# Retention and feed-forward on one core: earlier PE transposes, twelve PE-turned units in the output bank, half-tile stores from the ScalarE queue

## The chip, the cores and the metric

The kernel runs on one core of a Trainium2 chip. The metric is the device time of one execution in microseconds (us). The kernel before took 355.55 us (median of 3 runs, 354.68 to 355.61). One further execution was recorded by the hardware profiler; every duration below comes from that one.

Engine names are those of the profile: PE is TensorE's matmul, PEld its weight load, DVE is VectorE, ACT is ScalarE, POOL is GpSimd, and SP is SyncE, which here only starts transfers. An engine name with a q (SPq, POOLq) stands for that engine's instruction queue.

## The reference

Two operators run one behind the other. The first is a causal linear attention with a decay per head (8 batches, 8 heads, 576 positions, 64 dims); the second is a feed-forward layer with an ELU between its two products:

```
ret = (q @ k.T / sqrt(64)) * gamma_h ** (i - j)   for j <= i, else 0
x   = ret @ v                     # 4608 tokens x 512
h   = x @ w_in                    # 512 -> 2048
g   = where(h > 0, h, exp(min(h, 0)) - 1)
out = g @ w_out                   # 2048 -> 512
```

Inputs, weights and output are float32 in DRAM. The kernel multiplies in bfloat16 and accumulates in float32.

## The kernel before

**Units.** The 4608 tokens are cut into 36 units of 128 tokens; a pair of batches is nine units, and u % 9 tells whether a unit starts a batch (0), straddles two (4) or ends one (8). Per unit the attention does the following. Three loads on SP's queue (`load`; six smaller ones where u % 9 is 4) bring q, k and v. `cast` makes q and k bfloat16 (tile qkn), and `scale_v` on POOL multiplies v by the key side of the decay (tile vn). `turn` brings q and k into the transposed layout (tile qkT): for units below `PE_TURNED` by eight PE transposes into a PSUM tile tr, copied out half by DVE and half by ACT, and for the others by one transposing DMA on SP's queue. `scores` (16 matmuls into the one bank sc), `masks` on DVE (sc to pt), `inter` and `intra` (both into the one bank o), `state` (bank st) and `state_out` (ACT, tile sb, which the next unit's `inter` reads) finish the attention; `put_x` on DVE scales bank o into the group's tile xt. `stretch(u)` issues `scores` of unit u+1, then `inter`, `state`, `intra` of u, `masks` of u+1, `put_x` and `state_out` of u.

**Groups.** The feed-forward part works on groups of units: units 0 to 3, then 4 and 5, then 6 and 7, then seven groups of four. `ffn1` takes one group and one block of hidden columns: PE into a bank (three banks with the tag ph, or the one bank pm where told so), ACT computes the exponential (tile e), POOL subtracts 1 (tile m), DVE takes max and min with the bank's content (tile g). Only then is the bank free. `ffn2` sums 16 blocks of g into bank pm, ACT copies it out and SP stores it. For group 0 alone `ffn2_half` does this in eight half tiles of 256 columns, since the weights arrive in halves.

**Order.** The order on every engine is that of the code; nothing reorders it. The parts are: a loop over units 0 to 3 with dummy matmuls between its steps (`dummy`); `ffn1` of group 0; eight `ffn2_half` with the attention of units 4 and 5 between them; a loop of eight `ffn1` of group 1 with units 6 and 7; and from g = 2 on a merged sequence of `ffn1` of group g and `ffn2` of group g-1, with a `stretch` at four places.

**Queues around the change.** In the loop over units 0 to 3 each unit's steps follow each other: cast, transposes, scores, masks, `intra`. Loads of units 4 to 7 are issued on SP inside `ffn1` of group 0, and the half-tile stores (L351) stand behind them on the same queue. The copies of half tiles out of PSUM (L350) use three output buffers (opool, tag ot), so the fourth copy waits for the first store to land. Transposing DMAs stand on SP's queue from unit 8 on.

## Time and profile before

| | |
|---|---|
| three runs, median (lowest to highest) | 355.55 us (354.68 to 355.61) |
| profiled execution | 354.05 us |
| its span in the trace | 352.3 us |
| PE busy | 314.5 us, 89% of the span |
| DVE, POOL, ACT busy | 191.5, 137.5, 130.9 us |
| transfers | 49.73 MB, mean 141 GB/s |

The span is what the trace shows from the first to the last instruction; the 1.75 us by which the execution is longer lie around it. PE's busy share is 90% or more in most of the 40 slices of the page, and lower between about 50 and 115 us; there the time before and behind a matmul has to be read, not the share. The table of stages (first group of rows below) cuts the span at the starts of the kernel's parts: 0 to 26.9 is the loop over units 0 to 3, 26.9 to 40.7 `ffn1` of group 0, 40.7 to 50.3 five half tiles of `ffn2`, 50.3 to 58.6 a stretch without PE work, 58.6 to 71.8 the other half tiles with units 4 and 5, 71.8 to 89.2 `ffn1` of group 1 with units 6 and 7, 89.2 to 114.7 the merged sequence for g = 2, and the rest the sequences for g = 3 to the end. In the rows of a timeline the first number is the start, the second the time taken, and brackets hold how long the engine had been idle before and what ended that.

### The profile page before, as it was taken

To read this page: it belongs to the slowest core of one execution; us is meant where nothing else is said; L and a number is where in the kernel's file an instruction comes from. 1 tells how busy PE (TensorE), PEld (TensorE's weight loads), DVE (VectorE), ACT (ScalarE), POOL (GpSimd) and SP (SyncE) were. 2 spreads that over 40 slices of the span, in tenths; PEclk is the share of its full clock that TensorE was granted. 3 is DMA by queue.
4 is the path that set the end of the run, shared out by engine and by line. 5 is a ranking of instruction groups with operands and counts; after the bars stand their busy time and mean duration, and the time that the engine had idled before them with its cause. 6 is when DMAs were issued, how large, how long until landed. Compare 5 with 4: busy or idle time off the path is not lost.

```text
span 352.3 us, 7014 instructions
## 1 busy us (share of the span) xinstructions
PE 314.5 (89%) x2746; PEld 164.7 (47%) x2782; DVE 191.5 (54%) x286; ACT 130.9 (37%) x234; POOL 137.5 (39%) x205
## 2 busy tenths in 40 slices
PE   8889973866975999999899989998999999999995
PEld 3444562755554444444444444443454444444442
DVE  2545701547466688566666656565657465444400
ACT  5325502334221454433334334433443344344411
POOL 4585521036233655434344433443344332333300
PEclk9999996989996999999999999999999999999999
DMA  9999997723999989876958794879677221000021
GB/s 174 185 156 199 195 204 159 154 72 76 206 198 224 198 183 188 175 172 150 179 137 160 167 187 121 180 152 191 139 160 152 60 68 54 31 30 32 30 89 60
DMA packets 154144, 49.73 MB, mean 141 GB/s; under 512 B 142848, under 2 KB 150016, under 8 KB 154112
## 3 DMA queue, kind: packets, MB, share of 16 engines
q1 hardware_dynamic: 147840, 45.10, 61.8%
q0 software_dynamic: 6272, 4.19, 8.2%
q8 instruction: 21, 0.34, 0.5%
q14 instruction: 11, 0.09, 0.1%
HBM read 36.70 MB, written 9.44 MB: 131 GB/s over the span
## 4 chain that ended last, share of the span: by engine, by line
PE 28%; issue 27%; POOL 15%; DVE 14%; DMA 6%; SPq 6%; ACT 1%; POOLq 0%; DVEq 0%; ACTq 0%
POOL m L311 12%; PE pm L326 12%; PE ph L304 9%; SPq L85 5%; DMA rv<-in_v_dram 5%; DVE pt L212 5%; PE dum L359 4%; DVE qkn L166 4%; POOL vn L175 3%; DVE g L313 3%; DVE xt L276 2%; DMA rqk<-in_k_dram 1%; PE sc L203 1%; SPq L191 1%; ACT qkT L189 1%
## 5 line engine op out<-in xcount | busy, mean ns | idle before, releaser
L313 DVE SCALAR_TENSOR_TENSOR g<-ph,m 128x512 bf16<-128x512 f32 x144 | 98.6, 689 | 98.8 <-POOL m L311 98.6
L311 POOL TENSOR_SCALAR m<-e 128x512 bf16<-128x512 f32 x144 | 89.7, 624 | 159.1 <-ACT e L309 156.6
L304 PE MATMUL ph<-xt,w_in_sb 128*128 128x512 bf16 (+1 forms) x619 | 144.4, 361 | 6.9 <-DVE xt L276 5.7
L309 ACT ACTIVATE e<-ph 128x512 f32<-128x512 f32 x144 | 86.0, 597 | 144.1 <-PE ph L304 142.5
L326 PE MATMUL pm<-w_out_sb,g 128*128 128x512 bf16 x501 | 127.6, 381 | 4.5 <-DVE g L313 2.6
L304 PEld LDWEIGHTS <-w_in_sb 128*128 128x128 bf16 x640 | 61.5, 99 | 68.0 <-issue 8.2
L326 PEld LDWEIGHTS <-g 128*128 128x128 bf16 x512 | 49.7, 98 | 62.2 <-issue 4.2
L175 POOL TENSOR_TENSOR vn<-rv,gk 128x512 bf16<-128x512 f32 x36 | 37.7, 1048 | 29.3 <-DMA rv<-in_v_dram 23.1
L212 DVE TENSOR_TENSOR pt<-sc,mask 128x1024 bf16<-128x1024 f32 x36 | 43.7, 1215 | 8.1 <-PE sc L203 8.1
L166 DVE CAST qkn<-rqk 128x1024 bf16<-128x1024 f32 x28 | 24.3, 867 | 9.5 <-DMA rqk<-in_k_dram 6.1
L276 DVE TENSOR_TENSOR xt<-o,gx 128x512 bf16<-128x512 f32 x36 | 24.4, 679 | 2.9 <-PE o L263 2.9
L203 PE MATMUL sc<-qkT 64*64 64x128 bf16 x576 | 15.3, 225 | 11.2 <-DMA qkT<-qkn 5.1
L336 ACT COPY ot<-pm 128x512 f32<-128x512 f32 x31 | 18.1, 585 | 16.9 <-PE pm L326 16.7
L203 PEld LDWEIGHTS <-qkT 64*64 64x64 bf16 x576 | 9.6, 107 | 25.9 <-issue 7.8
L359 PE MATMUL dum<-warm 128*128 128x512 bf16 x58 | 17.5, 438 | 1.9 <-DVE warm L108 1.3
L255 ACT CAST sb<-st 128x256 bf16<-128x256 f32 x32 | 11.9, 372 | 19.3 <-PE st L246 19.3
L345 PE MATMUL pmh<-w_out_sb,g 128*128 128x256 bf16 x128 | 15.9, 284 | 0.5 <-DVE g L313 0.5
L263 PE MATMUL o<-pt,vn 128*64 128x128 bf16 x288 | 14.7, 224 | 0.0
L345 PEld LDWEIGHTS <-g 128*128 128x128 bf16 x128 | 12.8, 102 | 3.0 <-DVE g L313 0.8
L187 PE MATMUL tr<-ident,qkn 128*128 128x128 bf16 x64 | 5.5, 231 | 8.3 <-ACT qkn L169 8.3
L229 PE MATMUL o<-qkT,sb 64*64 64x128 bf16 (+1 forms) x256 | 12.5, 217 | 0.3 <-DVE xt L276 0.2
L263 PEld LDWEIGHTS <-vn 128*64 128x64 bf16 x288 | 9.5, 112 | 2.2 <-issue 1.7
(42 smaller groups left out, 74.9 us busy)
## 6 DMA issues: line engine op xcount, KB each, us to landing
rqk<-in_q_dram SPq DMA_DIRECT2D x32, 256.0 KB, 3.7
rqk<-in_k_dram SPq DMA_DIRECT2D x32, 256.0 KB, 4.4
rv<-in_v_dram SPq DMA_DIRECT2D x32, 256.0 KB, 4.6
out_dram<-ot SPq DMA_DIRECT2D x32, 256.0 KB, 2.0
w_in_sb<-in_moe_w_in_dram POOLq DMA_DIRECT2D x4, 512.0 KB, 8.4
w_out_sb<-in_moe_w_out_dram POOLq DMA_DIRECT2D x4, 512.0 KB, 15.9
rqk<-in_q_dram SPq DMA_DIRECT2D x8, 128.0 KB, 4.2
rqk<-in_k_dram SPq DMA_DIRECT2D x8, 128.0 KB, 4.4
```

The costliest lines, as they stand in the source:

```text
L166: engs[0](n, src)
L175: nc.gpsimd.tensor_tensor(n, rv, gk[:, u % R].unsqueeze(2).to_broadcast([P, H, D]), ALU.mult)
L203: nc.tensor.matmul(sc[j * 64 : (j + 1) * 64, i, hp], t[r, 1, hp, j * 64 : (j + 1) * 64], t[r, 0, hp], start=(hp == 0), stop=(hp == HP - 1) ...
L212: nc.vector.tensor_tensor(pt.rearrange("p i h t -> p (i h) t"), scs[u].rearrange("p i h t -> p (i h) t"), m.unsqueeze(1).to_broadcast([P, ...
L276: nc.vector.tensor_tensor(xts[g][:, :, i * P : (i + 1) * P], os_[u], gx[:, :, s0 : s0 + P], ALU.mult)
L304: nc.tensor.matmul(ph[:, i * n : (i + 1) * n], w_in_sb[:, j, f : f + P], xts[g][:, j, :n], start=(j == 0), stop=(j == KJ - 1), skip_group_ ...
L309: nc.scalar.activation(e, ph, AF.Exp)
L311: nc.gpsimd.tensor_scalar(m, e, -1.0, 1.0, ALU.add, ALU.mult)
L313: nc.vector.scalar_tensor_tensor(gt_, ph, 0.0, m, ALU.max, ALU.min)
L326: nc.tensor.matmul(pm, gts[g, ft][:, it * P : (it + 1) * P], w_out_sb[:, ft], start=(ft == 0), stop=(ft == NFT - 1))
L345: nc.tensor.matmul(pm, gts[g, ft][:, it * P : (it + 1) * P], w_out_sb[:, ft, c * 256 : c * 256 + 256], start=(ft == 0), stop=(ft == NFT - 1),)
L359: nc.tensor.matmul(dum, warm[:, :P], warm, start=True, stop=True)
```

## The change

- In the loop over units 0 to 3 the next unit's casts and transposes stand between the current unit's `masks` and `intra`; there are fewer dummies. The four exponentials that make gx (`make_gx`) follow unit 0's casts on ACT. A one-element copy `seen` on POOL reads unit 3's q ahead of the first weight load.
- Units 4 to 11 (before: units 4 to 7) are turned on PE, and their tile tr now takes the one bank o instead of a ph bank (units 0 to 3 keep ph).
- Loads of units 4 to 11 (before: 4 to 7) are issued in one go.
- Half-tile stores and the stores of groups 1 and 2 go from SP's queue to ACT's; there are five output buffers instead of three.
- Units 4 to 11 are placed anew among the feed-forward steps.

```
-    PE_TURNED = 8
+    PE_TURNED = 12
...
-    opool = ctx.enter_context(tc.tile_pool(name="opool", bufs=3))
+    opool = ctx.enter_context(tc.tile_pool(name="opool", bufs=5))
...
-    for hp in range(HP):
-        nc.scalar.activation(gx[:, hp, :S], px, AF.Exp, bias=bx, scale=lgx[:, hp : hp + 1])
-    nc.gpsimd.tensor_copy(gx[:, :, S:], gx[:, :, 0:64])
+
+    def make_gx():
+        for hp in range(HP):
+            nc.scalar.activation(gx[:, hp, :S], px, AF.Exp, bias=bx, scale=lgx[:, hp : hp + 1])
+        nc.gpsimd.tensor_copy(gx[:, :, S:], gx[:, :, 0:64])
...
-    def turn(u):
+    def turn(u, bank=None):
...
-            ps = ps_h.tile([P, 2, HP, P], BF16, name="tr", tag="ph")
+            pool, tag = bank or (ps_o, "o")
+            ps = pool.tile([P, 2, HP, P], BF16, name="tr", tag=tag)
...
-            nc.sync.dma_start(out[i0 : i0 + P, :], ot)
+            (nc.scalar if g < 3 else nc.sync).dma_start(out[i0 : i0 + P, :], ot)
...
-        nc.sync.dma_start(out[u * P : (u + 1) * P, c * 256 : c * 256 + 256], ot)
+        nc.scalar.dma_start(out[u * P : (u + 1) * P, c * 256 : c * 256 + 256], ot)
...
-    nload = [8]
+    nload = [12]
...
     dummy(18)
+    cast(0, A, V)
+    make_gx()
+    scale_v(0)
+    turn(0, (ps_h, "ph"))
+    dummy(2)
     for u in range(4):
-        cast(u, A, V if u == 0 else G)
-        if u == 3:
-            load_w_in(0)
-        scale_v(u)
-        turn(u)
-        dummy(3)
         scores(u)
         inter(u)
         state(u)
-        dummy(5)
         masks(u)
+        if u < 3:
+            if u == 2:
+                G(seen, raws[3][0][0:1, 0, 0, 0:1])
+                load_w_in(0)
+            cast(u + 1, A, A if u == 2 else G)
+            scale_v(u + 1)
+            dummy(3)
+            turn(u + 1, (ps_h, "ph"))
+        else:
+            dummy(4)
         intra(u)
-        dummy(3)
         put_x(u)
         state_out(u)
+        dummy(2)
...
         if ft == 5:
             load(4, nc.vector)
-            load(5)
-            load(6)
-            load(7)
+            for u in range(5, 12):
+                load(u)
...
     prep(5, A, V)
     ffn2_half(1, 1)
     scores(4)
+    inter(4)
+    state(4)
     masks(4)
+    ffn2_half(2, 1)
+    intra(4)
+    put_x(4)
+    state_out(4)
     turn(5)
-    load_next()
-    load_next()
-    ffn2_half(2, 1)
-    stretch(4)
+    ffn2_half(3, 1)
+    scores(5)
     prep(6, A, V)
-    ffn2_half(3, 1)
+    inter(5)
+    state(5)
+    masks(5)
+    dummy(4)
+    intra(5)
+    put_x(5)
+    state_out(5)
     turn(6)
-    stretch(5)
     for i in range(8):
         ffn1(1, 2 * i, (ps_m, "pm") if i % 4 == 3 else None)
         if i == 0:
             prep(7, A, V)
+            scores(6)
+            masks(6)
+        if i == 1:
+            inter(6)
+            state(6)
+            intra(6)
+            put_x(6)
+            state_out(6)
         if i == 2:
             turn(7)
...
+    turn(8)
...
+        if g == 2:
+            at = [5, 9, 12, 14]
         for n, (what, gg, s) in enumerate(seq):
...
+            if g == 2 and n in (3, 7, 10):
+                turn(nxt[0] + 1)
             if nxt and n in at:
                 u = nxt.pop(0)
-                prep(u + 3, V)
+                prep(u + 2, V) if u < 10 else None
+                if u >= 9:
+                    prep(u + 3, V)
                 load_next()
                 stretch(u)
```

Three places show what this moves. The names are those of the code above; a row is one instruction, with x for equal ones in a row.

The first place is DVE in the loop over units 0 to 3, from unit 0's copy of tr on. Before:

```order
L188 COPY qkT<-tr 128x512
L212 TENSOR_TENSOR pt<-sc,mask 128x1024
L276 TENSOR_TENSOR xt<-o,gx 128x4x128
L188 COPY qkT<-tr 128x512
L212 TENSOR_TENSOR pt<-sc,mask 128x1024
```

And after:

```order
L191 COPY qkT<-tr 128x512
L215 TENSOR_TENSOR pt<-sc,mask 128x1024
L191 COPY qkT<-tr 128x512
L279 TENSOR_TENSOR xt<-o,gx 128x4x128
L215 TENSOR_TENSOR pt<-sc,mask 128x1024
```

The next unit's copy of tr (second L191) moved ahead of the current unit's `put_x` (L279).

The second place is the half-tile stores. Before, they stand on SP behind the loads of unit 7:

```order
L85 DMA rqk<-in_q_dram 128x8x64
L85 DMA rqk<-in_k_dram 128x8x64
L85 DMA rv<-in_v_dram 128x8x64
L351 DMA out_dram<-oth 128x256 x6
L85 DMA rqk<-in_q_dram 128x8x64
```

After, they stand on ACT between its copies and casts. This piece starts behind the sixteen exponentials of group 0; in brackets is what an instruction waits for, where DMAHW is the count of transfers that share one of eight semaphores:

```order
L354 DMA out_dram<-oth 128x256 [waits DMAHW3_49,DVE_49]
L353 COPY oth<-pmh 128x256 [waits PE_49]
L354 DMA out_dram<-oth 128x256 [waits DMAHW5_49,Activation_49]
L354 DMA out_dram<-oth 128x256 [waits DMAHW7_49,DVE_49]
L353 COPY oth<-pmh 128x256 [waits PE_49]
L354 DMA out_dram<-oth 128x256 [waits DMAHW1_49,Activation_49]
L171 CAST qkn<-rqk 128x512 [waits DMAHW4_49]
L354 DMA out_dram<-oth 128x256 [waits DMAHW3_49,DVE_49]
L192 COPY qkT<-tr 128x512 [waits DVE_49]
```

The stores no longer follow the loads, but unit 4's cast of q (L171) and its copy of tr (L192) now follow four and five stores on ACT, and each store waits for an earlier transfer of the same semaphore.

The third place is DVE in the sequence for g = 2, around `stretch(9)`. Before, one cast precedes each `masks`:

```order
L313 SCALAR_TENSOR_TENSOR g<-ph,m 128x512
L166 CAST qkn<-rqk 128x1024
L212 TENSOR_TENSOR pt<-sc,mask 128x1024
L276 TENSOR_TENSOR xt<-o,gx 128x4x128
```

After, unit 9's `put_x` (second L279 below) stands behind two casts and unit 10's `masks`:

```order
L279 TENSOR_TENSOR xt<-o,gx 128x4x128
L316 SCALAR_TENSOR_TENSOR g<-ph,m 128x512
L191 COPY qkT<-tr 128x512
L316 SCALAR_TENSOR_TENSOR g<-ph,m 128x512
L168 CAST qkn<-rqk 128x1024 x2
L215 TENSOR_TENSOR pt<-sc,mask 128x1024
L279 TENSOR_TENSOR xt<-o,gx 128x4x128
L316 SCALAR_TENSOR_TENSOR g<-ph,m 128x512
L191 COPY qkT<-tr 128x512
```

The last L191 is the copy of unit 11's tr; its transposes on PE write bank o, which the `put_x` ahead of it has to read first.

## Rows read from the trace of the kernel before

**Rows 1.** Stages: length; busy PE, PEld, DVE, ACT, POOL (xcount); clock, DMA share, GB/s.
```profile
0.00:26.90 26.90, 23.05 (x242) 11.45 (x247) 11.58 (x36) 10.47 (x18) 15.20 (x29) 1.00 1.03 172
26.90:40.70 13.80, 13.72 (x63) 6.26 (x64) 9.10 (x15) 8.92 (x15) 8.63 (x14) 1.00 1.38 196
40.70:50.30 9.60, 9.06 (x81) 7.64 (x79) 3.16 (x6) 1.00 (x3) 2.28 (x3) 1.00 1.21 194
50.30:58.60 8.30, 0.04 (x1) 0.00 (x0) 0.18 (x1) 0.89 (x2) 2.08 (x2) 0.77 1.01 209
58.60:71.80 13.20, 10.83 (x168) 8.79 (x169) 7.32 (x12) 4.28 (x9) 0.00 (x0) 0.89 0.66 143
71.80:89.20 17.40, 13.11 (x143) 9.63 (x143) 9.91 (x15) 6.45 (x12) 8.72 (x11) 0.90 0.33 74
89.20:114.70 25.50, 18.85 (x247) 12.85 (x250) 15.39 (x20) 6.47 (x12) 9.05 (x12) 0.87 1.15 209
114.70:352.30 237.60, 225.87 (x1805) 108.06 (x1830) 134.87 (x183) 92.44 (x164) 91.49 (x135) 1.00 0.58 127
```

**Rows 2.** Timeline, 43 to 60 us: SP's last loads and first stores, and who waits.
```profile
47.55 1.04 POOL L175 TENSOR_TENSOR vn<-rv,gk 128x512 bf16<-128x512 f32 x1 [5.26 <-DMA rv<-in_v_dram]
...
53.79 9.38 SPq L351 DMA_DIRECT2D out_dram<-oth  x6
54.08 1.04 POOL L175 TENSOR_TENSOR vn<-rv,gk 128x512 bf16<-128x512 f32 x1 [1.92 <-DMA rv<-in_v_dram]
57.67 0.37 ACT L350 COPY oth<-pmh 128x256 f32<-128x256 f32 x1 [12.16 <-DMA out_dram<-oth]
...
58.62 1.03 PE L187 MATMUL tr<-ident,qkn 128*128 128x128 bf16 x8 [8.28 <-ACT qkn L169]
...
59.45 2.95 PE L345 MATMUL pmh<-w_out_sb,g 128*128 128x256 bf16 x16
...
63.14 1.91 PE L345 MATMUL pmh<-w_out_sb,g 128*128 128x256 bf16 x16
```

**Rows 3.** The w_out loads' line: first and last start, time to landing.
```profile
L100 POOL DMA_DIRECT2D w_out_sb<-in_moe_w_out_dram x4: 913/918/933, 21.2 to 23.8; - x4
...
DMA to landing us min/median/max: 13.0/15.9/20.6
```

**Rows 4.** Timeline of one unit in the loop over units 0 to 3.
```profile
14.22 0.42 PE L203 MATMUL sc<-qkT 64*64 64x128 bf16 x16 [0.49 <-ACT qkT L189]
...
14.69 1.23 DVE L212 TENSOR_TENSOR pt<-sc,mask 128x1024 bf16<-128x1024 f32 x1 [1.14 <-PE sc L203]
...
16.36 0.61 POOL L169 CAST qkn<-rqk 128x512 bf16<-128x512 f32 x1 [1.35 <-DMA rqk<-in_k_dram]
...
17.23 0.61 PE L187 MATMUL tr<-ident,qkn 128*128 128x128 bf16 x8
...
18.97 0.26 PEld L203 LDWEIGHTS <-qkT 64*64 64x64 bf16 x16 [0.98 <-ACT qkT L189]
```

**Rows 5.** Timeline, 87 to 115 us: PE's waits for a bank and for a transposing DMA.
```profile
87.45 1.89 PE L326 MATMUL pm<-w_out_sb,g 128*128 128x512 bf16 x7 [2.56 <-DVE g L313]
...
89.62 1.05 PE L304 MATMUL ph<-xt,w_in_sb 128*128 128x256 bf16 x8
...
109.17 0.64 PE L203 MATMUL sc<-qkT 64*64 64x128 bf16 x16 [5.05 <-DMA qkT<-qkn]
```

**Rows 6.** Groups by line over the span: busy, mean ns | idle before, releasers.
```profile
L313 DVE SCALAR_TENSOR_TENSOR g<-ph,m 128x512 bf16<-128x512 f32 x144 | 98.6, 689 | 98.8 <-POOL m L311 98.6
L311 POOL TENSOR_SCALAR m<-e 128x512 bf16<-128x512 f32 x144 | 89.7, 624 | 159.1 <-ACT e L309 156.6 <-DVE g L313 2.5
...
L166 DVE CAST qkn<-rqk 128x1024 bf16<-128x1024 f32 x28 | 24.3, 867 | 9.5 <-DMA rqk<-in_k_dram 6.1 <-DMA rqk<-in_q_dram 3.4
...
L189 ACT COPY qkT<-tr 128x512 bf16<-128x512 bf16 x8 | 4.7, 585 | 13.4 <-DVE qkT L188 13.4
...
L188 DVE COPY qkT<-tr 128x512 bf16<-128x512 bf16 x8 | 3.4, 422 | 5.7 <-PE tr L187 5.7
```

More of the change, by code (lines that the diff above doesn't have):

```diff
@@ L350, in ffn2_half @@
         (nc.scalar.copy if u % 2 else nc.vector.tensor_copy)(ot, pm)
-        nc.sync.dma_start(out[u * P : (u + 1) * P, c * 256 : c * 256 + 256], ot)
+        nc.scalar.dma_start(out[u * P : (u + 1) * P, c * 256 : c * 256 + 256], ot)
     V, A, G = nc.vector.tensor_copy, nc.scalar.copy, nc.gpsimd.tensor_copy
-    dum = ps_m.tile([P, 512], FP32, name="dum", tag="pm")
     def dummy(n):
+        dum = ps_m.tile([P, 512], FP32, name="dum", tag="pm")
         for _ in range(n):
@@ L374, in load_next @@
             nload[0] += 1
+    seen = const.tile([1, 1], FP32, name="seen")
     dummy(18)
-    for u in range(4):
-        cast(u, A, V if u == 0 else G)
-        if u == 3:
-            load_w_in(0)
-        scale_v(u)
-        turn(u)
-        dummy(3)
+    cast(0, A, V)
[3 more added lines that the diff above has]
+    dummy(2)
+    for u in range(4):
         scores(u)
@@ L426 @@
             prep(7, A, V)
+            scores(6)
[6 more added lines that the diff above has]
+            state_out(6)
         if i == 2:
             turn(7)
-        if i == 3:
-            stretch(6)
-            prep(8, V)
-            load_next()
-        if i == 5:
-            prep(9, V)
-            load_next()
-        if i == 7:
-            stretch(7, ahead=False)
-            prep(10, V)
-            load_next()
+        if i == 4:
+            scores(7)
+            masks(7)
+            prep(8, A, V)
+        if i == 6:
+            stretch(7, ahead=False)
+            prep(9, A, V)
+            load_next()
+    turn(8)
     for g in range(2, NG + 1):
@@ L457 @@
         at = [n for n, (what, gg, s) in enumerate(seq) if what and s % 4 == 3]
-        if g in (2, 3):
+        if g == 3:
             at = [len(seq) * (i + 1) // 4 - 1 for i in range(4)]
         at[-1] -= 3
+        if g == 2:
+            at = [5, 9, 12, 14]
         for n, (what, gg, s) in enumerate(seq):
```

## The prediction

> **What bounds the kernel now.** I read the table of stages first, since PE's share over the whole span hides where it waits. [rows 1] shows two kinds of stage. From 114.7 us to the end PE is busy 225.87 of 237.6 us at clock 1.00: PE sets the time, and the change touches this part only in its first stores. The seven stages ahead of that, 114.7 us, hold 88.7 us of PE work, some of it dummies and some at a low clock (0.77 to 0.90 in four of them). Everything the change can win lies there.
>
> Next I read the timeline where PE does nothing at all, 50.3 to 58.6 us. [rows 2]: PE's transposes of unit 4 wait 8.28 us for ACT's cast of unit 4's q. That cast has had its data since about 47.5 us (POOL scales unit 4's v, the last of its loads, at 47.55), but ACT works in order and stands at a half-tile copy, which waits 12.16 us for an output buffer. The buffer is freed by the first half-tile store, and SP issues that store at 53.79 only, behind the loads of unit 7. So a queue's order makes the hole, no amount of work.
>
> Then the loop over units 0 to 3. [rows 4]: from one scores (14.22) to the next (18.97) are 4.75 us, and what ends last is serial: scores, masks 1.23 us, `intra`, transposes at 17.23, two copies one behind the other (ACT's copy waits for DVE's each time: [rows 6], 13.4 us in 8), scores.
>
> Last, 71.8 to 114.7 us. [rows 5]: PE waits 2.56 us for bank pm (DVE's g frees it), and 5.05 us at 109.17 for a transposing DMA while the transfers are saturated (DMA share 1.15 in that stage, after 0.33 in the one before, [rows 1]).
>
> **The change, stage by stage.** Sums run against the profiled execution, 354.05 us with a span of 352.3.
>
> *Units 0 to 3.* The first scores stay where they are: the 18 dummies still stand ahead of unit 0's transposes, and the exponentials for gx end before ACT has to copy these. With the next unit's transposes under the masks a period becomes, on PE, scores 0.42, `inter` and `state` (half as many matmuls each) 0.35 each, three dummies 0.65 (13.8 us / 64 = 0.216 for a 128x512 matmul, [rows 1]), transposes 0.61: 2.4 us; then DVE's copy 0.42, ACT's copy 0.59 and hops of 0.1: 3.5 us instead of 4.75. The masks fit beside it (0.47 + 1.23 = 1.7). Three periods save 3.75, the shorter last unit 0.2. `ffn1` of group 0 starts at 22.9 instead of 26.9. The loads don't forbid it: unit 3's k is there at 16.4 ([rows 4], the cast that waited for its DMA), and unit 3's transposes come at 18. **-4.0** (bounds -3 to -4.8). `seen` makes POOL wait for unit 3's q, but POOL's next work waits for unit 3's v, which lands later: nothing; were it not so, the weights come late by a POOL step of 0.6 us.
>
> *`ffn1` of group 0 and five half tiles.* Same PE work, 13.8 + 9.6 us: they end at 46.3. The last weights landed at 44.4 (23.8 + 20.6, [rows 3]) and are needed from 45 on; the loads of units 4 to 11 now start 4.2 us earlier against them, so this is tight. **0** (bounds 0 to +2).
>
> *The hole.* The stores leave SP's order, and five buffers let the fourth copy go without any store. What is late next is unit 4 itself: its v landed at 47.55, with the transfers saturated (DMA share 1.21 to 1.38, [rows 1]), and beginning earlier gains little on a full path. Units then land every 3.3 us (unit 4's v used at 47.55, unit 6's at 54.08: [rows 2]). Against 46.3 I leave 1.5 us of the 8.3: **-6.8** (bounds -8.3, if unit 4 is there in time, to -3.3, if the early loads of units 5 to 7 and six stores of 128 KB hold it up). Each store also occupies ACT while it is issued; SP took 9.38 us for six, waits for their copies included, so at most 1.6 us for one. ACT hides that: it is busy 1.00 of 9.6 us in the stage of the five half tiles ([rows 1]). Without this cover eight issues would cost up to 12 us, which is rival D.
>
> *The other half tiles, units 4 and 5.* Three half tiles of 1.9 us, three turns (units 4, 5 and 6; 0.6 each, the last beside `put_x`), two attentions (scores 0.42, the other three steps 0.4 at most: 1.5 each), and at the end, with nothing beside them, unit 5's masks, and `put_x`, a DVE pass over the same elements as g (0.69): 5.7 + 1.2 + 3.0 + 1.2 less 0.6 for the steps under the masks + 0.7 = 11.2 instead of 13.2 us. 1.0 of it is the half tile that ran at a low clock right after the hole (2.95 against 1.91 us, [rows 2]). **-2.0** (bounds -2.6 to +1, where unit 5 or 6 lands late).
>
> *Group 1 with units 6 and 7.* PE work: 8 `ffn1` x 1.05, two attentions 3.1, two turns 1.2, two `ffn2` pieces 1.9: 14.6 us. The waits come from DVE, which serves g, casts, masks, `put_x` and now copies of tr. `intra` of unit 6 waits for masks behind a g and a cast (1.5), scores and `intra` of unit 7 wait 0.4 and 0.6, the transposes of unit 8 wait for unit 7's `put_x` in bank o (1.0), and bank pm for the last g (0.6). Together 18.6 us against 17.4: **+1.2** (bounds -2 to +3).
>
> *Sequence for g = 2.* Gone: the wait of 5.05 us for a transposing DMA, since units 8 to 11 need none and their loads fell into earlier stages. In its place PE transposes three times in bank o, where it waits for `put_x` of the unit before. PE work: 8 x 1.05 + 6 x 0.9 + four stretches 5.4 + scores 0.4 + three turns 1.8 = 21.4 us. Waits: unit 10's transposes for unit 8's `put_x` 1.0. Unit 11's transposes wait longest: from the end of `put_x` of unit 8, DVE does g 0.69, copy 0.42, g 0.69 (for which it waits some 2 us, since ACT's exponential and POOL's m of 0.62 come behind a `ffn1` that PE starts late), two casts of 0.87, masks 1.23, `put_x` 0.69, in all 7.5 us with hops, while PE has 4.8 us of work (0.6 + 1.05 + 0.9 + 1.2 + 1.05): 2.7. Then 0.9 at bank sc and o for unit 11 and 1.3 before group 3's first `ffn1`. Together 27.3 us against 25.5: **+1.8** (bounds -3 to +4). What such a bank costs no row before shows; the 2.56 us of [rows 5] for bank pm is nearest to the 2.7 that I take.
>
> *From 114.7 on.* Same instructions in the same order, loads equally far ahead; four stores of units 4 to 7 stand on ACT, beside 92 us of ACT's work in 237. **0** (bounds -0.5 to +1).
>
> Sum: -4.0 - 6.8 - 2.0 + 1.2 + 1.8 = -9.8, so 344.25 as a profiled execution. The median of the three runs lies 1.5 us above the profiled one, their lowest 0.6 above; I add about 1 and forecast 345 us.
>
> **Rule against the rows.** SP issues the first store at 53.79, after the loads ahead of it, while ACT has been waiting for that store for most of 12.16 us [rows 2]; by these rows another queue frees the store. The Trainium skill, page "DMA: Bandwidth & Descriptors", section "Issuing engines are not separate DMA queues", says that transfers started by different engines run on the same 16 DMA engines and interleave, so a second issuing engine saves issue time only. By that rule little of the 8.3 us would come back: with -1.5 in place of -6.8, some 350 us. The rows show what it leaves out, the place in an in-order queue.
>
> **Rivals.**
> (B) The bank waits of the two stages after 71.8 don't bite: DVE runs ahead, both stages take their PE work and half the waits (16.6 and 24.4 us). Then -5 more: 340 us. For it: DVE is busy only 9.91 of 17.4 and 15.39 of 25.5 us there [rows 1]. Against: the waits are chains, not load.
> (C) Transfers are the bound from 30 to 60 us: their share is above 1 already, and now eight units, weights and stores come at once. Weights +2, hole -3.3, next stage +0.5 instead of 0, -6.8, -2.0 lose 8 us of the gain: 353 us; half of that, 349. This is the mechanism for which the page above speaks.
> (D) Slower: ACT becomes the queue in which things stick. Each store on ACT waits for an earlier transfer of its semaphore, and unit 4's cast and copy stand behind it. If these transfers are loads of late units, ACT stands until they land: unit 8 lands at 54.1 + 2 x 3.3 = 60.7, unit 11 at 70.6. Transposes of unit 4 at 71 instead of 58.6 make +12.4; with -2.0 + 3.0 behind it 367 us. It decides against the change from about 57.5 us of landing on. Against it: counted through by their semaphores in the order after, the first store follows a load of unit 3, and the second to fourth follow loads of unit 4, which its cast has to wait for anyway.
> (E) The gain in the first units is eaten by the wait for weights and the hole closes only in part, 354.5 to 356.5 us.
>
> **How the numbers follow.** The forecast (own range 341 to 348.5) has 0.55, B (334 to 341) 0.18, C (348.5 to 354) 0.18, D 0.06, E 0.03. The likeliest's bounds and the near halves of B and C give 337.5 to 351, which leaves out the far end of B, the worst of C, D and E, 2 in 10. A measurement of this kernel tells about 0.3% (1.1 us) from no change. Faster: 0.55 + 0.18 + 0.17 = 0.90; same: E and a rest of C, 0.04; slower: 0.06.
>
> **What would show it.** Right: in the timeline after, `ffn1` of group 0 starts near 22.9 us with scores every 3.5 us; the transposes of unit 4 follow the fifth half tile within 2 us; no copy of a half tile waits for a store; group 1's `ffn1` starts at 57 to 60; PE waits for DVE's xt (`put_x`) ahead of the transposes of units 8, 10 and 11; the last part takes 237 to 238 us. Wrong: ACT idle before a store for several us (D), PE waiting for loads in the half tiles or at units 5 and 6 (C), or the two stages behind group 1's start taking under 41 us together (B). The forecast fails if the last part isn't the same length.

## The result, and the profile after

The changed kernel takes 345.73 us (median of 4 runs, 345.54 to 346.47), beside 355.12 us for the kernel before on the same chip: a ratio of 0.9741, 95% interval 0.9716 to 0.9765. That is faster, by 9.4 us; the forecast was 345.0, range 337.5 to 351. The profiled execution took 345.76 us with a span of 344.1, so the span is 8.2 us shorter than before.

The stages of the changed kernel, as [rows 1] has them of before (length; busy PE, PEld, DVE, ACT, POOL; clock, DMA share, GB/s). The cuts are at the same places: start of `ffn1` of group 0, first half tile, end of the fifth one, transposes of unit 4, `ffn1` of group 1, `scores(8)`, group 3. Two of them are early here: the first half tile starts at 36.93, not 36.46, and the fifth ends at 46.75, not 46.10.

```profile
0.00:22.66 22.66, 18.86 (x225) 9.56 (x226) 11.42 (x36) 10.89 (x19) 12.24 (x27) 1.00 1.07 171
22.66:36.46 13.80, 13.50 (x62) 6.06 (x62) 8.57 (x14) 8.49 (x15) 10.78 (x17) 1.00 1.33 199
36.46:46.10 9.64, 9.05 (x79) 7.50 (x78) 3.09 (x6) 1.81 (x4) 1.53 (x3) 1.00 1.33 199
46.10:47.70 1.60, 0.65 (x6) 0.34 (x4) 0.85 (x2) 0.62 (x1) 1.01 (x1) 1.00 1.19 312
47.70:59.40 11.70, 10.04 (x156) 7.97 (x157) 5.77 (x9) 3.69 (x8) 2.14 (x3) 1.00 1.04 248
59.40:78.10 18.70, 13.36 (x176) 9.60 (x175) 11.50 (x18) 8.37 (x16) 8.14 (x11) 1.00 1.18 217
78.10:106.36 28.26, 20.41 (x273) 13.79 (x273) 18.51 (x24) 8.52 (x16) 10.57 (x13) 0.94 0.46 95
106.36:344.10 237.74, 228.06 (x1832) 108.16 (x1831) 134.12 (x182) 91.72 (x163) 90.75 (x134) 1.00 0.58 126
```

The stretch without PE work (8.30 us in [rows 1]) is 1.60 us long by these cuts, and PE works in 0.65 us of it. The loop is 4.3 us shorter, the stages with units 6 to 11 are longer (18.7 and 28.3 us instead of 17.4 and 25.5), and the last part is as long as before. The clock, which was 0.77 to 0.90 in four stages of before, is 1.00 in all but one.

The timeline around the former hole, which answers to [rows 2] (start, length, what; in brackets the idle time before and what ended it):

```profile
40.05 0.38 ACTq L354 DMA_DIRECT2D out_dram<-oth  x1
...
41.74 2.97 ACTq L354 DMA_DIRECT2D out_dram<-oth  x2
...
44.83 0.37 ACT L353 COPY oth<-pmh 128x256 f32<-128x256 f32 x1 [3.12 <-PE pmh L348]
...
46.14 0.43 DVE L171 CAST qkn<-rqk 128x512 bf16<-128x512 f32 x1 [2.63 <-DMA rqk<-in_k_dram]
...
46.69 1.04 POOL L177 TENSOR_TENSOR vn<-rv,gk 128x512 bf16<-128x512 f32 x1 [8.20 <-DMA rv<-in_v_dram]
46.69 0.34 ACTq L354 DMA_DIRECT2D out_dram<-oth  x1
...
47.07 0.62 ACT L171 CAST qkn<-rqk 128x512 bf16<-128x512 f32 x1 [1.87 <-DMA rv<-in_v_dram]
...
47.74 0.62 PE L190 MATMUL tr<-ident,qkn 128*128 128x128 bf16 x8 [0.99 <-ACT qkn L171]
```

The first store is issued at 40.05 instead of 53.79, and no copy of a half tile waits for a store. PE's transposes come 0.99 us after its last half tile, since ACT casts unit 4's q only at 47.07. That q had landed at 44.29 and ACT was free from 45.20 on, but the fourth store stands ahead of the cast on ACT, and it waits for an earlier transfer of its semaphore: the load of unit 4's v, which landed at 46.61 and which the cast does not need. DVE's half of the cast (unit 4's k, 46.14) ends before PE's fifth half tile does. E3, the changed kernel with its stores back on SP, has the same loads and no store on ACT; there the cast starts at 45.11 and the transposes wait for nothing:

```profile
45.11 0.62 ACT L171 CAST qkn<-rqk 128x512 bf16<-128x512 f32 x1
...
46.38 0.61 PE L190 MATMUL tr<-ident,qkn 128*128 128x128 bf16 x8
```

So what is left of the hole is ACT's order, and unit 4's v enters only through the store: it is used at 46.69, 0.9 us earlier than in [rows 2], although the first `ffn1` started 4.3 us earlier.

The loop over units 0 to 3, as in [rows 4]. Scores now start at 9.10, 12.10, 15.36 and 19.63. Unit 3's turn:

```profile
17.43 0.62 ACT L171 CAST qkn<-rqk 128x512 bf16<-128x512 f32 x1 [1.32 <-DMA rqk<-in_k_dram]
...
18.10 0.40 PE L190 MATMUL tr<-ident,qkn 128*128 128x128 bf16 x4 [0.83 <-ACT qkn L171]
...
19.63 0.42 PE L206 MATMUL sc<-qkT 64*64 64x128 bf16 x16 [0.25 <-ACT qkT L192]
```

Two periods take 3.0 and 3.26 us (4.75 in [rows 4]); the third takes 4.27, because unit 3's k is cast at 17.43 only, as soon as it has landed (16.36 in [rows 4]).

The places where PE waits longest in all (engine, line, for whom: us in total, times, longest). In the same view of before stand 8.3 us for ACT's cast ([rows 2]), 5.1 for the transposing DMA and 2.6 for bank pm ([rows 5]), and besides 5.7 for `put_x` ahead of an `ffn1` and 4.7 for ACT's copy of tr ahead of scores:

```profile
PE tr L190 <- DVE xt L279: 7.8, 5, 3.5
PE ph L307 <- DVE xt L279: 5.9, 7, 1.2
PE sc L206 <- ACT qkT L192: 2.7, 6, 0.9
PE o L266 <- DVE pt L215: 2.4, 2, 1.6
```

The first line is new, the second and third were there before. The new one is the one bank o, where a unit's transposes wait for `put_x` of the unit before. The longest of the five, on PE and then on DVE:

```profile
94.75 1.01 PE L190 MATMUL tr<-ident,qkn 128*128 128x128 bf16 x8 [3.54 <-DVE xt L279]
```

```profile
89.99 0.69 DVE L316 SCALAR_TENSOR_TENSOR g<-ph,m 128x512 bf16<-128x512 f32 x1 [1.85 <-POOL m L314]
90.60 2.37 DVE L168 CAST qkn<-rqk 128x1024 bf16<-128x1024 f32 x2
92.89 1.21 DVE L215 TENSOR_TENSOR pt<-sc,mask 128x1024 bf16<-128x1024 f32 x1
94.02 0.68 DVE L279 TENSOR_TENSOR xt<-o,gx 128x512 bf16<-128x512 f32 x1
```

DVE runs g, two casts, masks and `put_x` without a gap from 89.99 on, and PE stands until the last of them is done.

The waits of [rows 5]: that for a transposing DMA is gone, and the one for bank pm is down from 2.56 to 0.74 us. Of the groups in [rows 6], DVE's casts take longer each, 932 ns instead of 867 (busy, mean ns, idle before):

```profile
76.25 1.89 PE L329 MATMUL pm<-w_out_sb,g 128*128 128x512 bf16 x8 [0.74 <-DVE g L316]
```

```profile
L168 DVE CAST qkn<-rqk 128x1024 bf16<-128x1024 f32 x26 | 24.2, 932 | 0.0
```

### The profile page after: what moved, and what is told of

Same layout as the page of the kernel before. It is cut to its first block, busy times and chain, and to the rows that moved or that the text cites. A ratio compares the mean times of both kernels' runs of the same rounds, so it can differ in the third digit from the quotient of the medians.

```text
span 344.1 us, 7077 instructions
## 1 busy us (share of the span) xinstructions
PE 313.9 (91%) x2797; PEld 163.0 (47%) x2797; DVE 193.8 (56%) x290; ACT 134.1 (39%) x241; POOL 137.2 (40%) x205
## 4 chain that ended last, share of the span: by engine, by line
issue 31%; PE 22%; POOL 20%; DVE 12%; SPq 6%; DMA 6%; ACT 1%; POOLq 0%; DVEq 0%; ACTq 0%
POOL m L314 13%; PE pm L329 12%; PE ph L307 9%; SPq L85 6%; POOL vn L177 5%; DVE pt L215 4%; DVE qkn L168 3%; DMA rv<-in_v_dram 3%; DVE g L316 3%; DMA rqk<-in_k_dram 3%; DVE xt L279 2%; POOL w_out_sb L100 1%; POOL w_in_sb L95 1%; PE sc L206 0%; PE o L266 0%
## 5 line engine op out<-in xcount | busy, mean ns | idle before, releaser
L329 PE MATMUL pm<-w_out_sb,g 128*128 128x512 bf16 x512 | 129.7, 381 | 1.4 <-DVE g L316 0.7
L307 PEld LDWEIGHTS <-w_in_sb 128*128 128x128 bf16 x640 | 60.3, 98 | 68.1 <-issue 9.2
L279 DVE TENSOR_TENSOR xt<-o,gx 128x512 bf16<-128x512 f32 x36 | 24.4, 678 | 1.1 <-PE o L266 1.1
L168 DVE CAST qkn<-rqk 128x1024 bf16<-128x1024 f32 x26 | 24.2, 932 | 0.0
L190 PE MATMUL tr<-ident,qkn 128*128 128x128 bf16 x96 | 7.9, 226 | 9.6 <-DVE xt L279 7.8
L192 ACT COPY qkT<-tr 128x512 bf16<-128x512 bf16 x12 | 7.0, 585 | 22.7 <-DVE qkT L191 22.7
L348 PE MATMUL pmh<-w_out_sb,g 128*128 128x256 bf16 x128 | 15.0, 273 | 0.6 <-DVE g L316 0.5
L362 PE MATMUL dum<-warm 128*128 128x512 bf16 x45 | 13.8, 440 | 1.3 <-DVE warm L108 1.3
```

The costliest lines, as they stand in the source:

```text
L168: engs[0](n, src)
L279: nc.vector.tensor_tensor(xts[g][:, :, i * P : (i + 1) * P], os_[u], gx[:, :, s0 : s0 + P], ALU.mult)
L307: nc.tensor.matmul(ph[:, i * n : (i + 1) * n], w_in_sb[:, j, f : f + P], xts[g][:, j, :n], start=(j == 0), stop=(j == KJ - 1), skip_group_ ...
L329: nc.tensor.matmul(pm, gts[g, ft][:, it * P : (it + 1) * P], w_out_sb[:, ft], start=(ft == 0), stop=(ft == NFT - 1))
L348: nc.tensor.matmul(pm, gts[g, ft][:, it * P : (it + 1) * P], w_out_sb[:, ft, c * 256 : c * 256 + 256], start=(ft == 0), stop=(ft == NFT - 1),)
```

## Experiments

All kernels are held against stages with the same marks: start of `ffn1` of group 0; from there to the transposes of unit 4; to `ffn1` of group 1; to `scores(8)`; to the first row of eight 512-wide `ffn1` matmuls of group 3 (116.22 in before, 108.09 in after); and to the end of the span. Lengths in us from the profiled execution of each, the median over its timed runs, and its ratio to the runs of before on the same chip. A stage's length is from one execution: after, E5, E6 and E7 have the same code up to the transposes of unit 4, and their first two columns add up to between 47.28 and 48.22, so differences below 1 us in a single stage are not read here.

| kernel | loop | to tr(4) | to group 1 | to scores(8) | to group 3 | rest | median | ratio, interval |
|---|---|---|---|---|---|---|---|---|
| before | 26.93 | 31.69 | 13.20 | 17.45 | 26.95 | 236.1 | 355.12 | |
| after | 22.66 | 25.08 | 11.70 | 18.63 | 30.02 | 236.0 | 345.73 | 0.974 [0.972, 0.977] |
| E1 | 26.68 | 23.26 | 18.39 | 16.42 | 27.31 | 236.1 | 349.16 | 0.983 [0.979, 0.987] |
| E2 | 26.68 | 23.81 | 11.79 | 18.01 | 26.47 | 236.1 | 344.51 | 0.970 [0.967, 0.973] |
| E3 | 22.65 | 23.73 | 33.57 | 19.01 | 30.10 | 235.9 | 365.55 | 1.028 [1.025, 1.032] |
| E4 | 22.29 | 36.50 | 13.15 | 17.41 | 29.26 | 236.2 | 355.37 | 1.000 [0.998, 1.002] |
| E5 | 22.13 | 26.09 | 10.38 | 19.19 | 27.57 | 235.9 | 343.45 | 0.966 [0.963, 0.969] |
| E6 | 22.23 | 25.60 | 11.70 | 19.37 | 29.05 | 236.0 | 344.70 | 0.972 [0.969, 0.975] |
| E7 | 22.51 | 24.77 | 10.38 | 19.67 | 26.72 | 236.0 | 341.08 | 0.960 [0.957, 0.962] |
| E8 | 22.09 | 25.79 | 11.79 | 17.53 | 27.47 | 236.1 | 342.19 | 0.963 [0.962, 0.965] |
| E9 | 22.46 | 24.85 | 11.79 | 17.92 | 27.32 | 236.2 | 343.19 | 0.966 [0.964, 0.967] |
| E10 | 22.91 | 24.99 | 11.78 | 17.41 | 29.76 | 236.3 | 343.60 | 0.967 [0.966, 0.969] |
| E11 | 22.57 | 25.10 | 11.78 | 16.94 | 28.43 | 237.3 | 341.42 | 0.963 [0.959, 0.966] |
| E12 | 22.05 | 25.73 | 11.85 | 15.88 | 26.53 | 236.4 | 341.50 | 0.964 [0.961, 0.967] |

**What closed the hole (E1 to E4).** The theory: the stores' place in SP's order made it, and the other parts depend on it. The rivals: the number of buffers, or the shorter loop.

E1, the kernel before with five output buffers:

```
-    opool = ctx.enter_context(tc.tile_pool(name="opool", bufs=3))
+    opool = ctx.enter_context(tc.tile_pool(name="opool", bufs=5))
```

> The kernel before with five output buffers instead of three, stores still on SP. If the hole came from the buffer wait alone (theory: buffer and SP's order together), unit 4's transposes come at about 50.5 us instead of 58.6, but the sixth half tile then needs the first store to land (57.6 in the trace before), so ACT stops there and only the work that fits in between is won: 5 to 6.5 us less than before, about 349.5. If five buffers closed the hole for good: 7 to 8 us less. If the queue alone mattered: no change within 1 us.

E2, the kernel before with its half-tile stores on ACT's queue (three buffers):

```
-        nc.sync.dma_start(out[u * P : (u + 1) * P, c * 256 : c * 256 + 256], ot)
+        nc.scalar.dma_start(out[u * P : (u + 1) * P, c * 256 : c * 256 + 256], ot)
```

> The kernel before with the eight half-tile stores on ACT's queue and still three output buffers. If SP's order makes the hole, the first store lands some 4 us after its copy at 43.8, the fourth copy finds its buffer at about 48, and unit 4's transposes follow the fifth half tile within 1 or 2 us: 6 to 8 us less than before, about 348. If transfers share engines and a second queue saves only issue time: 0 to 2 us less.

E3, the changed kernel with that line put back on SP:

```
-        nc.scalar.dma_start(out[u * P : (u + 1) * P, c * 256 : c * 256 + 256], ot)
+        nc.sync.dma_start(out[u * P : (u + 1) * P, c * 256 : c * 256 + 256], ot)
```

> The changed kernel with the eight half-tile stores back on SP, five buffers kept. Theory: they stand behind the loads of units 4 to 11, the sixth half tile waits for the first store, which lands near 68 us, and ACT stops from about 50 to 68: 12 to 15 us more than the changed kernel, about 358 and so slower than before. Rival, buffers suffice: within 1.5 us of the changed kernel.

E4, the kernel before with nothing but the new loop over units 0 to 3 (`make_gx` and `seen` included):

```
     for u in range(4):
-        cast(u, A, V if u == 0 else G)
...
         masks(u)
+        if u < 3:
...
+            cast(u + 1, A, A if u == 2 else G)
+            scale_v(u + 1)
+            dummy(3)
+            turn(u + 1)
```

> The kernel before with only the new loop over units 0 to 3 (turns under the masks, gx behind the casts, seen). ffn1 of group 0 starts at 22.7 us, 4.2 us earlier. Theory: the hole swallows part of it, since its end hangs on SP's loads, which run on a full transfer path: first store issued some 2 us earlier, time 2 us less than before (1 to 3). Rival, the parts add up: 4.2 us less.

Where the stall stands in each: E1 (five buffers), E2 (stores on ACT), E3 (stores back on SP) and E4 (loop alone), from their timelines:

```profile
54.69 4.50 SPq L351 DMA_DIRECT2D out_dram<-oth  x6
...
58.47 0.37 ACT L350 COPY oth<-pmh 128x256 f32<-128x256 f32 x1 [6.32 <-DMA out_dram<-oth]
...
59.38 0.64 PE L203 MATMUL sc<-qkT 64*64 64x128 bf16 x16 [4.44 <-ACT qkT L189]
```

```profile
50.49 0.62 PE L187 MATMUL tr<-ident,qkn 128*128 128x128 bf16 x8 [0.40 <-ACT qkn L169]
```

```profile
66.35 1.09 SPq L85 DMA_DIRECT2D rv<-in_v_dram  x1
...
67.53 9.82 SPq L354 DMA_DIRECT2D out_dram<-oth  x8
...
71.53 0.37 ACT L353 COPY oth<-pmh 128x256 f32<-128x256 f32 x1 [22.94 <-DMA out_dram<-oth]
...
72.97 1.01 PE L190 MATMUL tr<-ident,qkn 128*128 128x128 bf16 x8 [21.43 <-DVE xt L279]
```

```profile
53.88 9.41 SPq L353 DMA_DIRECT2D out_dram<-oth  x6
...
57.84 0.37 ACT L352 COPY oth<-pmh 128x256 f32<-128x256 f32 x1 [16.14 <-DMA out_dram<-oth]
...
58.79 1.03 PE L189 MATMUL tr<-ident,qkn 128*128 128x128 bf16 x8 [12.22 <-ACT qkn L171]
```

Five buffers move the stall from the fourth copy to the sixth and save some 6 us, as expected. One word in one line (E2) brings the time to 344.5 us, as much as the whole change, where 348 was expected. By the table 7.9 us of it are the hole and 1.4 the half tiles behind it, which run at a granted clock of 1.00 instead of 0.89. The same word taken out of the change (E3) makes it slower than the kernel before by 2.5 to 3.2%: the changed kernel puts the loads of eight units ahead of the stores, so the first of them is issued at 67.53. The loop alone (E4) reaches `ffn1` at 22.29 and loses all of it again: the hole grows from 8.28 to 12.22 us, since its end hangs on SP's loads and not on PE. So the place of the stores in a queue is the cause, and the loop's 4 us are worth something only when it is gone (E8 below, with the stores on ACT, takes 2.3 us less than E2; it has the loop and also the five buffers). I had expected 2 us of them to come through on their own.

**The bank of the transposes (E5 to E7).** The theory: the new waits in the stages of units 5 to 11 come from tr taking the one bank o and, at unit 11, from DVE's chain in front of `put_x`. The rival: the waits only change their names. E5 gives tr a ph bank; E6 lets ACT share the casts of units 10 to 14; E7 does both.

```
E5, E7:
-            pool, tag = bank or (ps_o, "o")
+            pool, tag = bank or (ps_h, "ph")
E6, E7:
-                prep(u + 2, V) if u < 10 else None
+                es = (A, V) if g == 2 else (V,)
+                prep(u + 2, *es) if u < 10 else None
...
-                    prep(u + 3, V)
+                    prep(u + 3, *es)
```

> The changed kernel with the transposes of units 4 to 11 in a ph bank instead of bank o. PE's waits ahead of the transposes (7.8 us in all, up to 3.5 at unit 11) go. If bank o as such costs them: 5 to 7 us less than the changed kernel, about 340. Theory: behind the bank stands DVE's order (put_x behind casts and masks, then the copy of tr behind put_x), so the wait moves to scores and put_x of the next unit: 1 to 2.5 us less, about 344; and the ph banks lose a turn to ffn1, which may take some of it.

> The changed kernel with the casts of units 10 to 14 in the sequence for g = 2 split between ACT (q) and DVE (k), which takes 0.5 us from DVE for each of five casts, two of them ahead of unit 9's put_x. Theory, DVE's chain sets that stage: 2 to 2.5 us less than the changed kernel, about 343.5; PE's wait at unit 11's transposes falls from 3.5 to about 2.5. Rival, bank o sets it: at most 0.5 us less.

> Transposes in a ph bank and the casts of units 10 to 14 split between ACT and DVE. Theory: the two add up, since each shortens the same DVE chain at another place: 3 to 4.5 us less than the changed kernel, about 342. If one of them makes the other useless: no more than the better one alone.

PE's longest waits of E5, from the same view as above:

```profile
PE ph L307 <- DVE xt L279: 6.4, 8, 1.5
PE sc L206 <- ACT qkT L192: 4.7, 6, 2.4
PE o L266 <- DVE pt L215: 2.7, 2, 2.0
PE pm L329 <- DVE g L316: 1.9, 1, 1.9
```

In E5 the 7.8 us that transposes waited for `put_x` are gone, about 3 us of waits come back on ACT's copies and bank pm, and the time falls by 2.3 us, within the 1 to 2.5 that the theory expected. E6 alone is inconclusive by time (its interval overlaps that of after); its trace shows unit 11's wait at 3.00 instead of 3.54 us, where I had expected about 2.5. Together they give 341.08 us, clearly below E5: 4.7 us less than the changed kernel, more than the 2.3 and 1.0 of the two added. That the shared bank kept DVE's freed time from being used in E6 is my reading of the two numbers; no row shows it directly.

**What the rest of the change is worth (E8 to E12).** E8 is the kernel before with the new loop, half-tile stores on ACT and five buffers. It leaves out all the rest of the change: the new order of units 4 to 11, units 8 to 11 turned on PE, bank o for tr, the early loads of units 8 to 11, and the stores of groups 1 and 2 on ACT. E9 adds the loads of units 4 to 11 in one go, E10 also the stores of groups 1 and 2 on ACT.

```
E8, from E4:
-    opool = ctx.enter_context(tc.tile_pool(name="opool", bufs=3))
+    opool = ctx.enter_context(tc.tile_pool(name="opool", bufs=5))
...
-        nc.sync.dma_start(out[u * P : (u + 1) * P, c * 256 : c * 256 + 256], ot)
+        nc.scalar.dma_start(out[u * P : (u + 1) * P, c * 256 : c * 256 + 256], ot)
E9, from E8:
-    nload = [8]
+    nload = [12]
...
-            load(5)
-            load(6)
-            load(7)
+            for u in range(5, 12):
+                load(u)
...
-    load_next()
-    load_next()
E10, from E9:
-            nc.sync.dma_start(out[i0 : i0 + P, :], ot)
+            (nc.scalar if g < 3 else nc.sync).dma_start(out[i0 : i0 + P, :], ot)
```

> The kernel before with two parts of the change: the new loop over units 0 to 3, and the half-tile stores on ACT with five buffers. The loop alone gave nothing, the stores alone 344.5 us. Theory: the hole had swallowed the loop's 4.2 us; with the hole closed unit 4's landing (46.7 in the trace after) swallows some 1.3 of it, and the rest comes through: 2 to 3 us less than the stores alone, about 342, and so less than the whole change. Rival: transfers bound this stretch whatever PE does: no gain over the stores alone (344.5).

> As e8, and the loads of units 4 to 11 are issued in one go as in the change; units 8 to 11 still turned by DMA, groups 1 and 2 in the order before. Theory: the wait for a transposing DMA in the sequence for g = 2 (4.8 us with the stores alone) comes from the loads that crowd that stage, so with them issued earlier it falls to 2 us or less: 2 to 4 us less than e8, about 339. Rival: the wait is the transposing DMA's own time behind SP's order: no change against e8.

> As e9, with the stores of groups 1 and 2 on ACT too, as in the change. One of them stands on SP ahead of unit 12's transposing DMA (93.2 to 94.8 in the trace with the stores alone) and waits for ACT's copy. Theory: what is left of PE's wait for that DMA falls by 1.5 us: about 337.5. Rival: DMA landing sets it, no change against e9.

E8 took 342.19 us, as expected, and is 3.5 us faster than the changed kernel. By the table what it leaves out costs 1.1 us in group 1 and 2.6 us in the sequence for g = 2, although it removes the wait for a transposing DMA (4.7 us in E8). That is not the order alone: E5 takes 2.3 us off by the bank, and E7, which has the new order, is as fast as E8 within their intervals. My theory that early loads would take the wait away without PE's transposes fell: it stays 4.8 us in E9 and 4.28 in E10. Neither reached the expected 339 and 337.5 us; E10 is slower than E8 beyond their intervals. SP's queue in E10, ahead of that wait:

```profile
88.72 2.20 SPq L193 DMA_TRANSPOSE qkT<-qkn  x1
90.96 0.58 SPq L85 DMA_DIRECT2D rqk<-in_q_dram  x1
91.58 0.62 SPq L85 DMA_DIRECT2D rqk<-in_k_dram  x1
92.72 0.96 SPq L85 DMA_DIRECT2D rv<-in_v_dram  x1
...
93.81 3.22 SPq L193 DMA_TRANSPOSE qkT<-qkn  x1
...
99.35 0.64 PE L205 MATMUL sc<-qkT 64*64 64x128 bf16 x16 [4.28 <-DMA qkT<-qkn]
```

SP spends 2.2 to 3.2 us on a transposing DMA and 0.6 to 1.0 on each of the three loads behind it, and the scores start 5.5 us after the DMA's issue began. I read from it that SP's pace and the DMA's own time set the wait, not the unit's loads; no run tests this.

E11 is E7 with the order of E8 for units 4 to 7 (only units 8 to 11 newly turned on PE); E12 is E11 with the last `ffn1` of group 1 in a ph bank.

```
E11, from E7:
     scores(4)
-    inter(4)
-    state(4)
     masks(4)
+    turn(5)
     ffn2_half(2, 1)
-    intra(4)
-    put_x(4)
-    state_out(4)
-    turn(5)
+    stretch(4)
...
         if i == 0:
             prep(7, A, V)
-            scores(6)
-            masks(6)
...
-        if i == 4:
-            scores(7)
-            masks(7)
+        if i == 3:
+            stretch(6)
             prep(8, A, V)
...
+        if i == 7:
+            stretch(7, ahead=False)
E12, from E11:
-        ffn1(1, 2 * i, (ps_m, "pm") if i % 4 == 3 else None)
+        ffn1(1, 2 * i, (ps_m, "pm") if i == 3 else None)
```

> The changed kernel with its last first layer of each half unit in a ph bank and the conversions of units 10 to 14 split over ScalarE and VectorE (the version measured at 341.08 us), but with the order of the kernel before for units 4 to 7 and group 1: those four units are turned by the DMA engines again, all are stretched between the half tiles, and only units 8 to 11 are turned on TensorE. Theory (turning units 4 to 7 on TensorE buys nothing once the stores are off SP, and costs TensorE's instructions and the waits for the output bank): the stage of group 1 takes 14.6 to 15.5 us instead of 17.9, the stage of group 2 stays near 26.8 us, and the time is 339 to 340.5 us. Rival (what the turning of these units costs is paid by waits that stay, for a landing or for the pm bank): no gain, 341 us or more.

> The kernel of the run beside it, with the last first layer of group 1 in a ph bank instead of the pm bank. Theory: the wait of 1.9 to 2.6 us for the pm bank ahead of group 2's first matmuls goes and nothing is late behind it, 338 to 339 us. Rival: the next instructions of TensorE wait as long for a ph bank or for the turned tile of unit 8, the same time as the run beside it.

(E11's text is wrong in one thing: units 4 to 7 are turned on PE in both kernels before and after; what E11 restores is their place.) Both are the same as E7 within their intervals, so nothing is gained that the timed runs show, and the expected 339 to 340.5 and 338 to 339 us were not reached. The profiles show the stage of group 1 shorter, 16.94 and 15.88 us instead of 19.67, and the wait of 1.5 us for bank pm gone in E12, where 1.9 us of waits for a g ahead of a ph bank stand instead of 0.3. But these runs scatter with the clock: four of E11's and E12's twelve runs came at a mean clock of 0.985 and took 342.9 to 344.3 us, those at 0.997 and above 340.2 to 340.7, while E7's five runs came at 0.993 to 0.999. E12's one run at full clock, 340.20 us, lies below E7's best of 340.75, but on another chip, where before itself takes 354.64 us and not 355.50; as ratios the two are alike. Whether this order is better, or draws the low clock more often, stays open.

The best version by median is E7, 341.08 us: a ratio of 0.960 to the kernel before, with an interval clear of the changed kernel's.

## Why the prediction was right

*Loop over units 0 to 3.* Predicted -4.0, measured -4.27. Two periods came out below the 3.5 us that I had worked out, and the third above it (4.27), since it waited for unit 3's k. I had read from [rows 4] that this k would be there at 16.4, and it came at 17.4: issued at about the same time (11.13 us, 11.27 before), it landed after 6.3 us instead of 5.0. The first weight load is now issued at 15.18 instead of 16.91, ahead of that landing, because `seen` makes POOL wait for unit 3's q and not for its k. The longest landing of these loads is 6.1 us in E4 and E8, which have the new loop, and 5.2 in E2, which has not. That the weights' transfer held up k is my reading; no run moves `seen` alone.

*`ffn1` of group 0 and the five half tiles.* Predicted 0, measured +0.7: 24.1 us (22.66 to 46.75) instead of 23.4. Two terms show. The larger was put at nothing, POOL, which still issues the weights' loads:

```profile
21.60 3.54 POOL L100 DMA_DIRECT2D w_out_sb<-in_moe_w_out_dram  x4
25.11 2.50 POOL L314 TENSOR_SCALAR m<-e 128x512 bf16<-128x512 f32 x4
```

Before, these issues ended at 24.7, two us ahead of the first `ffn1`; now four m queue behind them, and PE waits 0.30 us for a g. The other is the weights' landing, which I had weighed. The last of them landed 21.5 us after its issue at 24.2, so at 45.7, in the middle of the fifth half tile, and PE's weight loads pause there:

```profile
45.72 0.75 PEld L348 LDWEIGHTS <-g 128*128 128x128 bf16 x7 [0.23 <-issue]
```

In E3, where the last weights came 0.4 us earlier, this pause is missing, and the last 65 matmuls of these half tiles take 7.27 us instead of 7.48. Of the +0.7 about 0.2 us are not traced.

*The hole.* Predicted 1.5 us left of 8.28, measured 0.99: with the term above, -6.6 for the two against -6.8. The reading of [rows 2] was right, and E2 and E3 show it from both sides. The reason given for what is left was not: I took it for unit 4's landing, but the cast's data were there, and ACT stood at the fourth store until unit 4's v had landed. That the size came out nearly right is luck.

*The other half tiles.* Predicted -2.0, measured -1.5 (11.70 us against 11.2). Two waits for bank o, 0.82 and 0.79 us at units 5 and 6, were not in the sum; E5 takes them out and the stage falls to 10.38.

*Group 1.* Predicted +1.2, measured +1.2. The wait for unit 7's `put_x` was 0.97 us (1.0 predicted), that for bank pm 0.74 (0.6), that of unit 6's `intra` 1.64 (1.5). That the sum agrees so well is in part luck: PE was busy 13.4 us and waited some 5.3, where I had 14.6 of work and 4.1 of waits.

*Sequence for g = 2.* Predicted +1.8, measured +2.9 (28.29 us, `scores(8)` to group 3). This is the mis-sized term. Unit 10's transposes waited 1.66 us (1.0 predicted), unit 11's 3.54 (2.7): DVE's chain from one `put_x` to the next took 7.7 us instead of 7.5, its two casts 2.37 us and not 1.74, beside POOL's scaling of two v tiles, and PE had 4.1 us of work beside it instead of 4.8. These two waits are 1.5 us longer than in the sum. Another 1.5 us were put at nothing: behind the wait, from 94.75 to 98.55, the granted clock was 0.58, and the transposes, four `ffn2` matmuls and one `ffn1` took 3.80 us up to the next scores, where the same steps behind unit 10's transposes took 2.27:

```profile
95.56 1.91 PE L329 MATMUL pm<-w_out_sb,g 128*128 128x512 bf16 x4
```

The miss is only 1.1 us because the work was put too high: 21.4 us, where PE was busy 20.4, low clock included.

*The rest.* Predicted 0, measured +0.1 (237.74 us).

The sum was -9.8 and is -8.2, or 345.76 as a profiled execution; that the median of the four runs lies at the profiled one, and not 1 us above it, made up for half of that 1.5 us, by chance.

*The rivals.* B fell: the waits for bank o bite. C's resource is real (the DMA share is 1.33 ahead of unit 4), but what late landings show here, 0.2 us at the last weights and about 1 us at unit 3's k, is not 4 to 8 us. D's mechanism is there and small. The row of 2.97 us at 41.74 holds two stores whose issue took 0.34 us each; the second of them waited for unit 4's q, while PE still had half tiles to do. The fourth store's wait is what is left of the hole. I had dismissed it because the cast needs the same loads, and that is so for q and k but not for v.

The same transfers issued by another engine are worth 10.9 us in E2 (355.43 to 344.51), because they leave an in-order queue: before, the fifteen loads of units 4 to 7 occupied SP from 34.43 to 53.69, and the stores came behind them. The Trainium skill, page "DMA: Bandwidth & Descriptors", section "Issuing engines are not separate DMA queues", says that starting transfers from several engines saves only the issuing engine's time for starting them, which is usually small; by this rule I had put some 350 us. Here the trace does not agree, since that time was 19 us on SP, and the measurement decides.

What the prediction did not see is how little of the gain is due to its parts by themselves. The terms were added as if independent. E4 shows the loop worth nothing without the stores. E8 shows that everything beyond loop, half-tile stores and buffers gives back 3.5 us, about a quarter of what these had won; the sum had it at +3.0 and so forecast a loss there without asking whether to leave it out.

## What to carry to other kernels

When a copy waits for a buffer whose store was issued late, look at what stands ahead of that store in its engine's order before anything else: here moving one line to another queue was worth the whole change. Time saved ahead of a stall that hangs on another engine's queue is not saved, so close the stall first and then shorten what leads to it. An engine that issues a store also stands at it until what the store waits for has landed, so look at what comes behind the store on that engine. Before giving a tile a bank that others use, write down who has to read the bank next and what stands ahead of that reader on its engine.

## What the runs showed of the hardware

A transposing DMA occupied SP for 1.23 us at least and up to 3.22 us in E10, with 3.0 to 6.4 us to its landing, while in the trace of before it was 1.24 to 2.30 and 3.0 to 4.6. I had taken its cost to be its landing alone.

Of before's casts on DVE of a whole unit, four ran with POOL idle and took 0.69 us each; most others, with POOL at work for part of the time, took 0.92, and the longest in the changed kernel, the second of the two ahead of unit 9's `put_x`, took 1.53 us with POOL busy throughout. In one case the cast kept its 0.69 us (at 107.19 in before), and POOL's scaling of v took 1.25 us instead of 1.04. No run tests this by itself.

The same 24 matmuls at the start of group 1 took these times in the profiled executions of E11 and then of E12:

```profile
59.45 4.45 PE L307 MATMUL ph<-xt,w_in_sb 128*128 128x256 bf16 x24 [1.23 <-DVE xt L279]
```

```profile
59.63 2.78 PE L307 MATMUL ph<-xt,w_in_sb 128*128 128x256 bf16 x24 [1.23 <-DVE xt L279]
```

From 59.5 to 72.0 the granted clock was 0.86 in E11, so partly the lower of the two levels, and 1.00 in E12. Ahead of it PE had the same instructions and was busy 9.93 and 10.23 of 13.5 us. Between such draws lie about 3 us of E11's and E12's times, as much as the smaller effects here; five or six timed runs did not settle them.
